# Later loads of s and b, first parts and splits of down 1 inside block 5, and a second product's weights in three steps, in an attention kernel with two FFNs

## The chip, the cores and the metric

The kernel runs on one core of a Trainium2 chip (trn2). The metric is device time in microseconds, the median of three runs. The profile and all rows below are of one further execution, taken by the hardware profiler.

## The reference

Chunked attention (4 batches, 8 heads, 768 tokens, chunks of 32 with 16 tokens to the left, 8 to the right and 8 memory tokens) gives a 3072 x 512 array. Two FFNs follow, the second one without a part in this change:

```python
h = x @ w_in                     # 3072x512 @ 512x2048
g = s * relu(h)**2 + b           # s and b are single numbers
x = g @ w_out                    # 3072x2048 @ 2048x512
h = x @ w2_in
x = (h - tanh(h)) @ w2_out
```

## The kernel before

**Stages.** Attention is done in 24 units of 128 tokens, and "up 1" (`x @ w_in`, relu, square, times `s`) in six blocks of 512 tokens with 16 tiles `t` each. The first two blocks and most of the attention stand in a hand-written order, the string `START`, whose tokens name a step and its index: `qk2` loads q and k of unit 2, `vv3` loads v of unit 3, `ra3` loads the raw weights 3 of `w_in` (64-bit numbers, which L131 to L145 turn into float32). The rest of up 1 is a loop over blocks `j` and tiles `t`. In both, each engine runs its instructions in the order in which the code issues them, and all DMAs go through one queue, SP's; a load on that queue also waits until the eighth load before it has landed.

**A tile of up 1** is 12 matmuls (`up1_products`), the relu on ScalarE (L398), and the square on VectorE (L408). After four tiles, `up1_combine` makes the sums that the next stage wants (four instructions of VectorE, L423) and `up1_store` writes all to DRAM.

**Down 1** (`g @ w_out`, the class `Down`) is a Strassen-like scheme of seven products P1, P6, P5, P7, P3, P2, P4. Each product has 12 entries, counted here from 0 at the first entry of P1, so that P6 begins with entry 12. An entry is 12 matmuls (`multiply`: two column groups, two row tiles, and three matmuls for each, since a float32 operand is held as a high and a low part: high times high, low weight times high, high times low). So an entry's third matmul is the first to need the low half of its data.

- A part is half of a product's data of a group of tokens, loaded from DRAM in two DMAs (L579); four buffers (`stream`). A part serves two entries.
- `split(i)` makes high and low of entry `i`: ScalarE adds `b` and writes the high half (L522), VectorE writes the low half (L523). Three buffers (`ring`), so `split(i + 2)`, which the code issues ahead of `multiply(i)`, can only start once entry `i - 1` is through. The ring lies where weights 4 and 5 of `w_in` and the high halves of block 5's input were; splits 0, 1 and 2 take these places in this order.
- `weights(p, half)` makes the weights of a product: up to two sums (L489, L504), the high half on ScalarE (L508), the low half (L509). For P6 all but the high half is done on VectorE, for the later products on GpSimd (POOL).
- `run` loads the first four parts, does splits 0 and 1, and then goes through the entries.

From entry 11 of P1 on, only TensorE's order is by hand; the other engines' order is set by a scheduler when the kernel is built.

Of the kernel before, what the change touches and what calls it, by code (L numbers as in the profile page):

```python
# [11 lines left out]
AF = mybir.ActivationFunctionType  # L12
# [5 lines left out]
P = 128  # L18
# [40 lines left out]
def tile_chunk_attention_two_ffn(  # L59
# [12 lines left out]
    nc = tc.nc  # L72
    NU = qk.shape[0]
    UB = NB // P
    NBLK = NT // NB
# [27 lines left out]
    def new(place, n, dt, name):  # L103
        assert n <= SIZE[place[0]], (place, n)
        if place[0] in "QSRY":
            assert place[0] in side["letters"], place
        pool = arena if place[0] in "EZ" else side["of"]
        return pool.tile([P, n], dt, tag=place, name=name)
# [12 lines left out]
    b_c = const.tile([P, 1], F32, name="b_c")  # L121
# [95 lines left out]
    def load_qk(u):  # L217
        qk_t[u] = new(A_QK0[u] if u < 5 else A_QK[(u + 1) % 3], 1280, F32, "qk")
        nc.sync.dma_start(out=qk_t[u], in_=qk[u])
# [45 lines left out]
    def divide(u):  # L265
        sm, sums = sm_t[u], sum_t.pop(u)
        rs = small.tile([P, 8, 1], F32, tag="rs", name="rs")
        nc.vector.tensor_scalar_add(sums, sums, 1e-9)
        nc.vector.reciprocal(out=rs.rearrange("p h o -> p (h o)"), in_=sums)
        nc.vector.tensor_tensor(out=sm, in0=sm, in1=rs.to_broadcast([P, 8, KE]), op=ALU.mult)  # L270
# [51 lines left out]
    def att_step(i):  # L322

        if i - 1 < NU:
            transposes(i - 1)
            copies(i - 1)
        if i - 2 < NU:
            values(i - 2)
            x_high(i - 2)
            if i + 1 < NU:  # L330
                load_v(i + 1)
        if i < NU:
            scores(i)
            if i + 3 < NU:
                load_qk(i + 3)
        if i - 2 < NU:
            x_low(i - 2)
        if i < NU:
            mask(i)
            maximum(i)  # L340
            exponentials(i)
# [45 lines left out]
    def up1_products(j, t, lo=0, hi=NB):  # L387

        n, i = t // 2, t % 2
        xh, xl = (x[:, :, lo:hi] for x in x_t[j])  # L390
        wh, wl = wi[1, n]
        ps = up_ps[j, t] = bank(5 + (16 * j + t) % 3)
        for c in range(KD):
            three(ps[:, lo:hi], wh[:, i, c, :], wl[:, i, c, :], xh[:, c, :], xl[:, c, :], c == 0, c == KD - 1)

    def up1_relu(j, t):
        r = up_r[j, t] = new(A_R[(16 * j + t) % 3], NB, F32, "r")
        nc.scalar.activation(out=r, in_=up_ps[j, t], func=AF.Relu)  # L398
# [14 lines left out]
    def up1_combine(j, q, half):  # L413
        combine(*(t.rearrange("p s k t -> p s (k t)") for t in oab[j, q]), nc.vector, half)

    def up1_store(j, q):
        oa, ob = oab.pop((j, q))
        nc.sync.dma_start(out=o1[j][:, q, 0:3], in_=oa[:, 1:4].rearrange("p s k t -> p s (k t)"))
        nc.sync.dma_start(out=o1[j][:, q, 3:7], in_=ob.rearrange("p s k t -> p s (k t)"))

    def combine(oa, ob, eng, half=None):

        sub = lambda o, x, y: eng.tensor_tensor(out=o, in0=x, in1=y, op=ALU.subtract)  # L423
        if half in (None, 0):
            sub(ob[:, 0], oa[:, 0], oa[:, 1])
            sub(ob[:, 1], oa[:, 2], ob[:, 0])
        if half in (None, 1):
            sub(ob[:, 2], oa[:, 2], oa[:, 0])
            sub(ob[:, 3], ob[:, 1], oa[:, 3])

    class Down:
# [48 lines left out]
                self.loaded += 1  # L480

        def weights(self, p, half, eng=nc.gpsimd):

            z = lambda k: self.z[k, half]
            name = ORDER[p]

            def combo(i, x, y, op):
                t = new(self.smap[i][half], 1024, F32, f"s{i}")
                eng.tensor_tensor(out=t, in0=x, in1=y, op=op)  # L489
                self.st[i, half] = t  # L490
                return t

            if name == "P1":
                src = z("A11")
            elif name == "P6":
                s1 = combo(0, z("A21"), z("A22"), ALU.add)
                src = combo(1, s1, z("A11"), ALU.subtract)
            elif name == "P5":
                src = self.st[0, half]
            elif name == "P7":  # L500
                src = combo(0, z("A11"), z("A21"), ALU.subtract)
            elif name == "P3":
                src = self.st[1, half]
                eng.tensor_tensor(out=src, in0=z("A12"), in1=src, op=ALU.subtract)  # L504
            else:
                src = z("A12" if name == "P2" else "A22")
            w = new(self.whl[p % 2][half], 2048, F32R, "whl")
            nc.scalar.activation(out=w[:, 0:1024], in_=src, func=AF.Copy)  # L508
            eng.tensor_tensor(out=w[:, 1024:2048], in0=src, in1=w[:, 0:1024].bitcast(F32), op=ALU.subtract)  # L509
            self.w[p, half] = tuple(  # L510
                w[:, 1024 * q:1024 * (q + 1)].rearrange("p (k m) -> p k m", k=4) for q in range(2)
            )
# [32 lines left out]
        def run(self, between):  # L545
            deep = len(self.stream)
            self.load_to(deep - 1)
            n = len(self.entries)
            for i in range(2):
                self.split(i)  # L550
            for i in range(n):
                if i + 2 < n:
                    self.split(i + 2)
                    if i % 2:
                        self.load_to(i // 2 + 1 + deep)
                self.multiply(i)
                p, k = divmod(i, 4 * NG)
                if p + 1 < 7 and k in (5, 9):
                    self.weights(p + 1, (k - 5) // 4, nc.vector if p == 0 and self.turn == 0 else nc.gpsimd)
                between(p, k)  # L560

    class Sums:
# [24 lines left out]
    def final1(name, g, ps):  # L587
# [29 lines left out]
        else:  # L617
# [3 lines left out]
    down1 = Down(  # L621
        wo1, Z1, B_S, B_WHL, B_STREAM, B_RING, load1,
        lambda part, e: part.rearrange("p (b k t) -> p b k t", b=2, k=4)[:, :, 2 * e:2 * e + 2].rearrange(
            "p b k t -> p b (k t)"
        ),
        lambda t: lambda k: t[:, :, HB * k:HB * (k + 1)],
        b_c[:, 0:1], final1, 0,
    )
# [14 lines left out]
    for token in START.split():  # L643
        name = token.rstrip("0123456789")
        steps[name](int(token[len(name):]))
        if token == "qk2":
            nc.sync.dma_start(out=s_c, in_=s.partition_broadcast(P))
            nc.sync.dma_start(out=b_c, in_=b.partition_broadcast(P))

    load_v(13)  # L650
    load_qk(15)
    load_v(14)
    load_qk(16)

    quads = []
    for j in range(2, NBLK):
        last = j == NBLK - 1
        for t in range(16):
            q, i4 = t // 4, t % 4
            step = i4 == 2 and not last  # L660
            if step:
                att_step(4 * j + 6 + q)
            if t in ((0, 5) if last else (0, 8)):
                quads.append(down1.load_quadrant(A_RAW[1 if last else q // 2]))
            up1_products(j, t)
            if t in ((4, 9) if last else (6, 14)):
                quads.pop().end()
            if step and 4 * j + 6 + q < NU:
                divide(4 * j + 6 + q)
            up1_relu(j, t)  # L670
            up1_square(j, t)
            if t in ((3, 8) if last else (4, 12)):
                quads[-1].begin()
            if last and t in (4, 10):
                down1.weights(0, t // 8, nc.vector)
                down1.load_to(t // 8)
            if i4 == 3:
                up1_combine(j, q, None)
                up1_store(j, q)

# [3 lines left out]
    def w2_load(n):  # L684
        w2[n] = load_raw(wi2, n, C_RAW[0])

    def w2_make(n):
        make_pair(w2.pop(n), C_Z, C_W[n % 2], 2, n)

    def between1(p, k):  # L690
        if p == 0 and k == 4 * NG - 1:
            region.close()
            region.enter_context(tc.manual_schedule(engines={nc.tensor.engine}))
        if p == 6 and k == 0:
            w2_load(0)
        if p == 6 and k == 6:
            w2_make(0)

    down1.run(between1)
    thunks = []  # L700

# [153 lines left out]
```

## Time and profile before

| | |
|---|---|
| median of 3 runs | 1096.37 us (1095.09 to 1096.51) |
| the profiled execution | 1096.79 us, of which the span of instructions is 1095.0 us |
| PE (TensorE) busy | 1064.3 us, 97% of the span, 6072 matmuls |
| DVE (VectorE) busy | 711.0 us, 65% |
| ACT (ScalarE) busy | 487.2 us, 44% |
| POOL (GpSimd) busy | 264.7 us, 24% |
| mean granted clock of TensorE | 0.995 |

The span is from the first instruction to the last. Shares are averages over stages that differ: what an engine limits has to be read from the stage.

### The profile page before, as it was taken

Reading aid. Unit: us, or ns where it says so; the run is one execution under the profiler, and the core shown is the slowest. Engines: PE = TensorE matmul, PEld = TensorE weight load, DVE = VectorE, ACT = ScalarE, POOL = GpSimd, SP = SyncE. Lnnn points to the kernel's source line nnn. Section 1 sums busy time; section 2 is a strip of 40 time slices with the busy share of each in tenths; the row PEclk is TensorE's granted clock in tenths of the full one; section 3 lists DMA queues with packets and bytes.
Section 4 is the critical chain, followed back from the end, with each engine's and each line's share of the span. In section 5 each row is a group of like instructions: output and inputs, shape, how many; then the busy total and the mean of one; then the engine's idle time right before and its main releaser. Section 6 shows DMA issues by size and latency. Waiting matters only on the chain.

```text
span 1095.0 us, 15206 instructions
## 1 busy us (share of the span) xinstructions
PE 1064.3 (97%) x6072; PEld 877.8 (80%) x6072; DVE 711.0 (65%) x742; ACT 487.2 (44%) x863; POOL 264.7 (24%) x164
## 2 busy tenths in 40 slices
PE   5899999999999889999999999999999999999998
PEld 4778888888888668888888888888888888888886
DVE  6897777777758596578779885323322566576654
ACT  6665564555523454445555333222222454444432
POOL 1000000000000061011101378655657951111100
PEclk8999999999999999999999999999999999999999
DMA  8874858666448745655565765555535966566751
GB/s 271 263 252 188 274 195 318 251 243 223 181 192 315 263 152 192 194 193 192 195 225 183 267 252 220 224 200 211 226 153 208 334 227 214 195 223 238 241 202 58
DMA packets 71687, 242.16 MB, mean 221 GB/s; under 512 B 5312, under 2 KB 5312, under 8 KB 61376
## 3 DMA queue, kind: packets, MB, share of 16 engines
q1 hardware_dynamic: 71616, 241.19, 61.7%
q8 instruction: 47, 0.77, 0.3%
q14 instruction: 24, 0.20, 0.1%
HBM read 146.80 MB, written 94.37 MB: 220 GB/s over the span
## 4 chain that ended last, share of the span: by engine, by line
PE 90%; DVE 4%; DMA 4%; issue 1%; ACT 0%; SPq 0%; DVEq 0%; ACTq 0%
PE pb L124 28%; PE pb L126 28%; PE pb L125 28%; DMA raw<-in_wi_dram 2%; DMA qk<-in_qk_dram 2%; PE pb L298 2%; PE pb L276 2%; PE pb L236 1%; DVE ringhringl L523 1%; DVE ob L423 1%; DVE oa L408 0%; DVE z L145 0%; DVE z L139 0%; DVE sm L270 0%; ACT z L131 0%
## 5 line engine op out<-in xcount | busy, mean ns | idle before, releaser
L126 PE MATMUL pb<-ringhringl,whl 128*128 128x512 f32 x560 | 219.7, 392 | 7.0 <-DVE ringhringl L523 7.0
L124 PE MATMUL pb<-ringhringl,whl 128*128 128x512 f32 x560 | 218.7, 391 | 1.7 <-ACT ringhringl L522 1.7
L125 PE MATMUL pb<-ringhringl,whl 128*128 128x512 f32 x560 | 218.6, 390 | 0.0
L528 DVE TENSOR_TENSOR ringhringl<-part,ringhringl 128x1024 fp32r<-128x1024 f32 x92 | 128.5, 1397 | 84.7 <-ACT ringhringl L527 84.7
L527 ACT ACTIVATE ringhringl<-part 128x1024 fp32r<-128x1024 f32 x92 | 97.7, 1062 | 135.6 <-PE pb L126 121.5
L124 PE MATMUL pb<-xh,w 128*128 128x512 f32 (+1 forms) x392 | 153.9, 393 | 2.3 <-DVE oa L408 2.2
L125 PE MATMUL pb<-xh,w 128*128 128x512 f32 (+1 forms) x392 | 151.3, 386 | 0.3 <-DVE w L378 0.3
L126 PE MATMUL pb<-xl,w 128*128 128x512 f32 (+1 forms) x392 | 151.3, 386 | 0.0
L126 PEld LDWEIGHTS pb<-ringhringl,whl 128*128 128x128 f32 x560 | 105.5, 188 | 32.1 <-DVE ringhringl L523 10.2
L768 DVE TENSOR_TENSOR oa<-pb,r 128x1024 f32<-128x1024 f32 x48 | 58.5, 1221 | 107.8 <-ACT r L767 103.6
L124 PEld LDWEIGHTS pb<-ringhringl,whl 128*128 128x128 f32 x560 | 105.5, 188 | 23.6 <-ACT ringhringl L522 2.1
L125 PEld LDWEIGHTS pb<-ringhringl,whl 128*128 128x128 f32 x560 | 105.4, 188 | 22.1
L504 POOL TENSOR_TENSOR s<-zq,s 128x1024 f32<-128x1024 f32 x4 | 12.5, 3114 | 383.1 <-DVE whl L509 383.0
L767 ACT ACTIVATE r<-pb 128x1024 f32<-128x1024 f32 x48 | 49.1, 1025 | 122.9 <-PE pb L126 122.4
L398 ACT ACTIVATE r<-pb 128x512 f32<-128x512 f32 x96 | 55.7, 592 | 100.1 <-PE pb L126 85.7
L523 DVE SCALAR_TENSOR_TENSOR ringhringl<-part,b_c,ringhringl 128x1024 fp32r<-128x1024 f32 x48 | 74.4, 1569 | 27.6 <-ACT ringhringl L522 27.6
L408 DVE SCALAR_TENSOR_TENSOR oa<-pb,s_c,r 128x512 f32<-128x512 f32 x96 | 70.1, 746 | 32.1 <-ACT r L398 32.1
L124 PEld LDWEIGHTS pb<-xh,w 128*128 128x128 f32 x392 | 73.6, 188 | 19.8 <-DVE oa L408 4.1
L125 PE MATMUL pb<-x2hx2l,w 128*128 128x512 f32 x224 | 87.2, 389 | 0.0
L126 PE MATMUL pb<-x2hx2l,w 128*128 128x512 f32 x224 | 87.2, 389 | 0.0
L124 PE MATMUL pb<-x2hx2l,w 128*128 128x512 f32 x224 | 87.2, 389 | 0.0
L260 ACT ACTIVATE sm<-sm,nmx 128x96 f32<-128x96 f32 x192 | 69.2, 365 | 37.7 <-DVE nmx L254 37.7
(108 smaller groups left out, 1818.0 us busy)
## 6 DMA issues: line engine op xcount, KB each, us to landing
o<-ob SPq DMA_DIRECT2D x48, 1024.0 KB, 4.7
part<-o SPq DMA_DIRECT2D x84, 512.0 KB, 4.6
part<-o SPq DMA_DIRECT2D x42, 1024.0 KB, 4.9
o<-oa SPq DMA_DIRECT2D x48, 768.0 KB, 3.4
raw<-in_wi_dram SPq DMA_DIRECT2D x16, 1024.0 KB, 6.6
raw<-in_wo_dram SPq DMA_DIRECT2D x16, 1024.0 KB, 7.2
qk<-in_qk_dram SPq DMA_DIRECT2D x24, 640.0 KB, 8.1
v<-in_vw_dram SPq DMA_DIRECT2D x24, 384.0 KB, 8.4
```

The lines of the kernel that those rows point to most:

```text
L124: nc.tensor.matmul(acc, lhsT=whi, rhs=xhi, start=first, stop=False)
L125: nc.tensor.matmul(acc, lhsT=wlo, rhs=xhi, start=False, stop=False)
L126: nc.tensor.matmul(acc, lhsT=whi, rhs=xlo, start=False, stop=last)
L260: nc.scalar.activation(out=sm[:, h, :], in_=sm[:, h, :], func=AF.Exp, bias=nmx[:, h:h + 1], scale=1.0, accum_out=sums[:, h:h + 1],)
L276: nc.tensor.transpose(out=bank(2 + g)[0:KE, P * r:P * (r + 1)], in_=sm[:, 4 * g + r, :], identity=ident)
L398: nc.scalar.activation(out=r, in_=up_ps[j, t], func=AF.Relu)
L408: nc.vector.scalar_tensor_tensor(out=oab[j, q][0][:, 2 * i:2 * i + 2, k, :], in0=ps2, scalar=s_c[:, 0:1], in1=r2, op0=ALU.mult, op1=ALU.mult,)
L523: nc.vector.scalar_tensor_tensor(out=xl, in0=src, scalar=self.bias, in1=xh.bitcast(F32), op0=ALU.add, op1=ALU.subtract)
L527: nc.scalar.activation(out=xh, in_=src, func=AF.Copy)
L528: nc.vector.tensor_tensor(out=xl, in0=src, in1=xh.bitcast(F32), op=ALU.subtract)
L767: nc.scalar.activation(out=r, in_=ps[:, :, 0:NB], func=AF.Tanh)
L768: nc.vector.tensor_tensor(out=oa[:, 2 * i:2 * i + 2], in0=ps[:, :, 0:NB], in1=r, op=ALU.subtract)
```

## The change

`s` is loaded behind v of unit 3 (so in front of v of unit 2), and `b` after the hand-written order. In the last block (block 5), parts 1 and 2 are loaded at tile 10 and part 3 at tile 11, and splits 0 and 1 are done at tiles 13 and 14. The block's last combine and store come after entry 0 of down 1, which is after split 2. P6's weights are made in three steps per half (`sums`, `high`, `low`), one entry apart, from entry 2 and from entry 6 on; before, all of a half came at entry 5 and at entry 9.

```diff
         def weights(self, p, half, eng=nc.gpsimd):
+            self.sums(p, half, eng)
+            self.high(p, half)
+            self.low(p, half, eng)
...
             self.load_to(deep - 1)
             n = len(self.entries)
             for i in range(2):
-                self.split(i)
+                if i not in self.xs:
+                    self.split(i)
...
                 p, k = divmod(i, 4 * NG)
-                if p + 1 < 7 and k in (5, 9):
-                    self.weights(p + 1, (k - 5) // 4, nc.vector if p == 0 and self.turn == 0 else nc.gpsimd)
+                if p == 0 and self.turn == 0:
+                    half = k // 6
+                    if k in (2, 6):
+                        self.sums(1, half, nc.vector)
+                    if k in (3, 7):
+                        self.high(1, half)
+                    if k in (4, 8):
+                        self.low(1, half, nc.vector)
+                elif p + 1 < 7 and k in (5, 9):
+                    self.weights(p + 1, (k - 5) // 4)
...
-        if token == "qk2":
+        if token == "vv3":
             nc.sync.dma_start(out=s_c, in_=s.partition_broadcast(P))
-            nc.sync.dma_start(out=b_c, in_=b.partition_broadcast(P))
...
     load_qk(16)
 
+    nc.sync.dma_start(out=b_c, in_=b.partition_broadcast(P))
...
                 down1.weights(0, t // 8, nc.vector)
-                down1.load_to(t // 8)
-            if i4 == 3:
+            if last and t in (4, 10, 11):
+                down1.load_to({4: 0, 10: 2, 11: 3}[t])
+            if last and t in (13, 14):
+                down1.split(t - 13)
+            if i4 == 3 and not (last and q == 3):
                 up1_combine(j, q, None)
                 up1_store(j, q)
...
     def between1(p, k):
+        if p == 0 and k == 0:
+            up1_combine(NBLK - 1, 3, None)
+            up1_store(NBLK - 1, 3)
```

How the engines' orders change, row by row. In these rows a line number is that of the file the rows are of: L523 (low half of a split) is L535 in the changed file, L489 (a sum) is L494, L504 (P3's sum) is L509, L509 (low half of weights) is L521. `x4` says that four such instructions follow one another.

VectorE from tile 12 of block 5 to entry 5 of down 1, before:

```order
L408 SCALAR_TENSOR_TENSOR oa<-pb,s_c,r 128x2x256 x4
L423 TENSOR_TENSOR ob<-oa 128x512
L423 TENSOR_TENSOR ob<-oa,ob 128x512
L423 TENSOR_TENSOR ob<-oa 128x512
L423 TENSOR_TENSOR ob<-ob,oa 128x512
L523 SCALAR_TENSOR_TENSOR ringhringl<-part,b_c,ringhringl 128x1024 x8
```

And now, from tile 12 to split 4:

```order
L408 SCALAR_TENSOR_TENSOR oa<-pb,s_c,r 128x2x256 x2
L535 SCALAR_TENSOR_TENSOR ringhringl<-part,b_c,ringhringl 128x1024
L408 SCALAR_TENSOR_TENSOR oa<-pb,s_c,r 128x2x256
L535 SCALAR_TENSOR_TENSOR ringhringl<-part,b_c,ringhringl 128x1024
L408 SCALAR_TENSOR_TENSOR oa<-pb,s_c,r 128x2x256
L535 SCALAR_TENSOR_TENSOR ringhringl<-part,b_c,ringhringl 128x1024
L423 TENSOR_TENSOR ob<-oa 128x512
L423 TENSOR_TENSOR ob<-oa,ob 128x512
L423 TENSOR_TENSOR ob<-oa 128x512
L423 TENSOR_TENSOR ob<-ob,oa 128x512
L535 SCALAR_TENSOR_TENSOR ringhringl<-part,b_c,ringhringl 128x1024 x2
```

Splits 0 and 1 now stand between the last squares, split 2 behind the last square, and the last combine between splits 2 and 3; before, all four instructions of the combine stood ahead of split 0.

VectorE over the entries of P1, before, from split 0 on:

```order
L523 SCALAR_TENSOR_TENSOR ringhringl<-part,b_c,ringhringl 128x1024 x8
L489 TENSOR_TENSOR s_3658<-zq 128x1024
L489 TENSOR_TENSOR s_3660<-s_3658,zq 128x1024
L509 TENSOR_TENSOR whl<-s_3660,whl 128x1024
L523 SCALAR_TENSOR_TENSOR ringhringl<-part,b_c,ringhringl 128x1024 x4
L489 TENSOR_TENSOR s_3733<-zq 128x1024
L489 TENSOR_TENSOR s_3735<-s_3733,zq 128x1024
L509 TENSOR_TENSOR whl<-s_3735,whl 128x1024
L523 SCALAR_TENSOR_TENSOR ringhringl<-part,b_c,ringhringl 128x1024 x6
```

And now, from split 3 on:

```order
L535 SCALAR_TENSOR_TENSOR ringhringl<-part,b_c,ringhringl 128x1024 x2
L494 TENSOR_TENSOR s_3605<-zq 128x1024
L494 TENSOR_TENSOR s_3607<-s_3605,zq 128x1024
L535 SCALAR_TENSOR_TENSOR ringhringl<-part,b_c,ringhringl 128x1024 x2
L521 TENSOR_TENSOR whl<-s_3607,whl 128x1024
L535 SCALAR_TENSOR_TENSOR ringhringl<-part,b_c,ringhringl 128x1024 x2
L494 TENSOR_TENSOR s_3680<-zq 128x1024
L494 TENSOR_TENSOR s_3682<-s_3680,zq 128x1024
L535 SCALAR_TENSOR_TENSOR ringhringl<-part,b_c,ringhringl 128x1024 x2
L521 TENSOR_TENSOR whl<-s_3682,whl 128x1024
L535 SCALAR_TENSOR_TENSOR ringhringl<-part,b_c,ringhringl 128x1024 x7
```

The second half's weights were done behind split 11 and are now done between splits 8 and 11, with splits 9 and 10 among their steps.

GpSimd's first instructions after its masks, of the second product (P6) and later, before and now, as one piece of the difference:

```order
-L504 TENSOR_TENSOR s_3660<-zq,s_3660 128x1024
-L509 TENSOR_TENSOR whl<-s_3658,whl 128x1024
-L489 TENSOR_TENSOR s_4089<-zq 128x1024
-L504 TENSOR_TENSOR s_3735<-zq,s_3735 128x1024
-L509 TENSOR_TENSOR whl<-s_3733,whl 128x1024
-L489 TENSOR_TENSOR s_4161<-zq 128x1024
+L509 TENSOR_TENSOR s_3607<-zq,s_3607 128x1024
+L509 TENSOR_TENSOR s_3682<-zq,s_3682 128x1024
+L521 TENSOR_TENSOR whl<-s_3605,whl 128x1024
+L494 TENSOR_TENSOR s_4089<-zq 128x1024
+L521 TENSOR_TENSOR whl<-s_3680,whl 128x1024
+L494 TENSOR_TENSOR s_4161<-zq 128x1024
```

These are P3's two sums (they work in place on P6's sums, so each must follow P6's low half), P5's low halves and P7's sums. Both of P3's sums now stand first.

## Rows read from the trace of the kernel before

**Rows 1.** Windows: core, stretch: us, busy us of each engine (instructions), clock, DMA share, GB/s.

```profile
150.00:300.00 150.00, 149.77 (x1278) 124.10 (x1277) 114.76 (x180) 78.34 (x257) 0.00 (x0) 1.00 0.68 247
365.00:367.70 2.70, 2.70 (x8) 2.08 (x8) 1.92 (x2) 0.00 (x0) 0.00 (x0) 0.55 0.98 250
```

**Rows 2.** What PE waited for, whole span: us in total, times, longest us.

```profile
PE pb L236 <- DMA qk<-in_qk_dram: 9.9, 6, 4.6
PE pb L126 <- DVE ringhringl L523: 7.0, 6, 3.0
```

**Rows 3.** Windows of the first 39 us, columns as in group 1.

```profile
7.00:10.00 3.00, 2.45 (x56) 1.93 (x48) 2.93 (x5) 1.66 (x9) 0.00 (x0) 1.00 0.26 87
12.40:22.60 10.20, 6.63 (x80) 5.30 (x80) 8.88 (x15) 8.45 (x32) 0.00 (x0) 0.84 1.03 306
22.60:38.70 16.10, 13.82 (x218) 12.50 (x219) 13.26 (x19) 10.49 (x28) 0.00 (x0) 0.89 1.02 281
```

**Rows 4.** Chain that ended last, 0 to 60 us: start us, us, what.

```profile
28.89 9.79 DMA raw<-in_wi_dram
```

**Rows 5.** Timeline of PE, block 5 to down 1: start us, us, instruction [idle before].

```profile
358.99 0.39 PE L126 MATMUL pb<-xl,w 128*128 128x512 f32 x1
361.10 0.50 PE L124 MATMUL pb<-ringhringl,whl 128*128 128x512 f32 x1 [1.73 <-ACT ringhringl L522]
...
364.58 0.80 PE L126 MATMUL pb<-ringhringl,whl 128*128 128x512 f32 x1 [2.74 <-DVE ringhringl L523]
...
367.61 0.39 PE L124 MATMUL pb<-ringhringl,whl 128*128 128x512 f32 x1
```

**Rows 6.** Timeline of PE, P1 to P6.

```profile
399.28 0.39 PE L125 MATMUL pb<-ringhringl,whl 128*128 128x512 f32 x1
402.66 0.50 PE L126 MATMUL pb<-ringhringl,whl 128*128 128x512 f32 x1 [2.99 <-DVE ringhringl L523]
...
405.29 0.39 PE L125 MATMUL pb<-ringhringl,whl 128*128 128x512 f32 x1
405.99 0.50 PE L126 MATMUL pb<-ringhringl,whl 128*128 128x512 f32 x1 [0.31 <-DVE ringhringl L523]
...
415.06 0.39 PE L124 MATMUL pb<-ringhringl,whl 128*128 128x512 f32 x1
```

**Rows 7.** Timeline of ACT, last tiles of block 5.

```profile
356.70 0.60 ACT L398 ACTIVATE r<-pb 128x512 f32<-128x512 f32 x1 [2.12 <-PE pb L126]
359.42 0.60 ACT L398 ACTIVATE r<-pb 128x512 f32<-128x512 f32 x1 [2.12 <-PE pb L126]
359.91 3.21 ACT L522 ACTIVATE ringhringl<-part,b_c 128x1024 fp32r<-128x1024 f32 x3
```

**Rows 8.** Timeline of DVE, end of block 5 into down 1.

```profile
357.33 0.75 DVE L408 SCALAR_TENSOR_TENSOR oa<-pb,s_c,r 128x512 f32<-128x512 f32 x1 [1.97 <-ACT r L398]
...
360.71 0.68 DVE L423 TENSOR_TENSOR ob<-oa 128x512 f32<-128x512 f32 x1
...
363.24 3.67 DVE L523 SCALAR_TENSOR_TENSOR ringhringl<-part,b_c,ringhringl 128x1024 fp32r<-128x1024 f32 x3
...
381.78 1.22 DVE L489 TENSOR_TENSOR s<-zq 128x1024 f32<-128x1024 f32 x1
```

**Rows 9.** DVE line L523: duration ns min/median/max, first and last start us.

```profile
L523 DVE SCALAR_TENSOR_TENSOR ringhringl<-part,b_c,ringhringl x48: 1271/1284/3442, 363.2 to 560.8; 128x1024 fp32r<-128x1024 f32 x48
```

**Rows 10.** Timeline of POOL, P1 to P6.

```profile
394.96 3.26 POOL L509 TENSOR_TENSOR whl<-s,whl 128x1024 fp32r<-128x1024 f32 x1 [4.87 <-ACT whl L508]
...
401.48 3.38 POOL L504 TENSOR_TENSOR s<-zq,s 128x1024 f32<-128x1024 f32 x1
```

**Rows 11.** POOL on tile zq, columns as in group 9.

```profile
L509 POOL TENSOR_TENSOR whl<-zq,whl x10: 2402/2511/3417, 499.1 to 1026.9; 128x1024 fp32r<-128x1024 f32 x10
```

**Rows 12.** Timeline of SP, the loads of down 1's parts.

```profile
346.18 0.88 SPq L579 DMA_DIRECT2D part<-o  x2
...
363.78 2.52 SPq L579 DMA_DIRECT2D part<-o  x3
```

More of the change, by code (lines that the diff above doesn't have):

```diff
@@ L482, in weights, with sums @@
         def weights(self, p, half, eng=nc.gpsimd):
+            self.sums(p, half, eng)
+            self.high(p, half)
+            self.low(p, half, eng)
+        def sums(self, p, half, eng):
             z = lambda k: self.z[k, half]
@@ L506, in weights, with high, low @@
                 src = z("A12" if name == "P2" else "A22")
+            self.w[p, half] = src
+        def high(self, p, half):
             w = new(self.whl[p % 2][half], 2048, F32R, "whl")
-            nc.scalar.activation(out=w[:, 0:1024], in_=src, func=AF.Copy)
+            nc.scalar.activation(out=w[:, 0:1024], in_=self.w[p, half], func=AF.Copy)
+            self.w[p, half] = (self.w[p, half], w)
+        def low(self, p, half, eng):
+            src, w = self.w[p, half]
             eng.tensor_tensor(out=w[:, 1024:2048], in0=src, in1=w[:, 0:1024].bitcast(F32), op=ALU.subtract)
```

## The prediction

> **What bounds the kernel now.** Read first the busy shares by stage. Between 150 and 300 us TensorE is busy 149.77 of 150 us [rows 1]: there the kernel is bound by matmuls, no edit touches that stage, and a shift of all that goes before it passes straight to the end. So the change can only work where TensorE waits. The list of its waits names two such places [rows 2]: 9.9 us for q and k at the start, and 7.0 us for the low halves of splits (`ringhringl`, L523) where down 1 begins. Then take each place from the timelines.
>
> Start. The queue of loads is what runs there: from 12.4 to 38.7 us the DMA engines are full (share 1.03 and 1.02). But from 7 to 10 us the share is 0.26 at 87 GB/s [rows 3], although the first three loads of q and k are all but through and large loads stand behind them; what lies between in the queue are `s` and `b`, a single number each, spread to 128 partitions. Against the 1.02 of the full stretch that hole is 3.0 x (1 - 0.26/1.02) = 2.2 us. The chain that ended last runs over the fourth load of raw weights, issued at 28.89 and 9.79 us under way [rows 4], so a full queue delays it, and behind it stand the conversions of weights that TensorE's first tiles need.
>
> Beginning of down 1. The last matmul of block 5 starts at 358.99; the next ten steps should take 10 x 0.227 = 2.27 us (a tile of 12 matmuls takes 2.72 us, by the relus of two tiles at 356.70 and 359.42 [rows 7]), but the tenth matmul from there starts at 367.61 [rows 5]. So 8.62 - 2.27 = **6.35 us** are lost. Why: ScalarE starts split 0 at 359.91, behind the last relu [rows 7]; VectorE first does the last square and the four instructions of the combine (from 360.71) and starts the low halves at 363.24 [rows 8]. The two idle gaps are 1.73 and 2.74 us [rows 5]; the rest is the clock, which fell behind these gaps: 0.55 granted between 365.0 and 367.7 [rows 1], about the lower of its two levels, 1.2 of 2.4 GHz.
>
> P1 to P6. From 367.61 (matmul 9 of down 1, counted from 0) to 415.06 (matmul 192, the first of entry 16) are 183 steps, 41.5 us at 0.2267, and 47.45 us pass [rows 5, 6]: **5.95 us** more are lost. The largest piece is entry 12: its second matmul starts at 399.28, the third, which needs the low half of its split, at 402.66 [rows 6]; on VectorE that split stands behind split 11 and the whole of P6's second half. Entries 13 to 15 lose about 0.6 us each in the same place (405.29 to 405.99, less a step and a little slow start [rows 6]), and entry 9 did once. Here VectorE and GpSimd hold each other up: a low half takes 1.28 us in the median but up to 3.44 [rows 9], and a tensor operation of GpSimd, 2.40 us at its shortest [rows 11], takes 3.26 to 3.38 [rows 10]. Five follow one another from 394.96, 3.34 us apart (one is that at 401.48); in each such period VectorE gets one operation, and TensorE wants a split every 2.72.
>
> **The change part by part, in the profiled execution's time (1096.79).**
>
> Start. The hole of `b` leaves the full stretch; its new place is near 160 us, where TensorE has loads in hand, so I cost it at nothing (if the cover were gone: 1.1 us). `s` stays in the full stretch, ahead of v of unit 2. Each had half of the hole, so q and k of unit 3 and the next loads come 2.2 us earlier, and what stands behind `s`, with the raw weights on the chain, 1.1 us. Bounds: 0 (something else made the hole, or it comes back whole) and 2.2 (in a queue with work on both sides a small load costs nothing). I take **1.1**, since the row shows the hole in just such a queue. On SP, v of unit 2 now waits also for the landing of the first raw weights; the queue is full long beyond that, so no cost.
>
> The Trainium skill speaks against this term: its page DMA: Bandwidth & Descriptors (Queues, rings and completion order) says that data descriptors of a ring are consumed in order and carry no barrier, so a load of 512 bytes should hardly hold what is behind it. By that the term would be 0 and the sum 1086.5; the row shows the engines idle, and I go by the row.
>
> Entry to down 1. In block 5 ScalarE idles 2.12 us per tile and VectorE 1.97 [rows 7, 8]; a split takes about 1.1 (a third of 3.21) on the one and 1.28 on the other, so splits 0 and 1 fit into tiles 13 and 14 at no cost. Count time T from the end of block 5's matmuls (359.2 before); entry i should start at 2.72 i, and its low half is due at 2.72 i + 0.45. Split 0 is then done at T = -2, split 1 at about 0.4 (due 3.2). Split 2 runs behind the last relu and square: high half to 1.7, low to 2.95, due 5.9. The combine (4 x 0.62 in a row) takes VectorE to 5.5, split 3 to 6.75, due 8.6. Parts 1 to 3 are issued from 346 on instead of 346.18 and 363.78 [rows 12], so none is late. No gap, so no fall of the clock either: **6.35** gained; at the least 4.47 (both gaps gone, the clock falls for another reason).
>
> P1 to P6. I carry the order on VectorE on, with 1.2 us per operation in a row (sums 1.22 [rows 8]); split i + 2 starts at 2.72 i at the earliest, and its high half takes 1.1 on ScalarE. Done / due: split 4 at 8.0 / 11.3; P6's first sums 10.4; split 5 at 11.7 / 14.0; split 6 at 15.4 / 16.8 (ScalarE has the high weights and P1's copy in between); low weights 16.6; split 7 at 17.8 / 19.5. Then GpSimd starts P3's first sum and holds split 8 to 21.1 / 22.2. Second sums 23.5, split 9 at 24.8 / 24.9, split 10 at 27.0 / 27.6, low weights 28.2, split 11 at 29.5 / 30.4. So entries 8 to 11 wait for nothing, two of them by a hair. At 28.3 GpSimd starts on five operations (P3's second sum, P5's two low halves and P7's two sums), and each split now comes 3.34 behind the last one: split 12 at 32.7 / 33.1, split 13 at 36.0 / 35.8, splits 14, 15 and 16 each 0.62 later than TensorE wants it. That is 0.2 + 3 x 0.6 = 2.0 us of waits where 5.95 were: **3.95** gained. Bounds: 5.95 (no waits left) and 2.5 (next paragraph's price of a period).
>
> With the shortest durations in the rows, one of each engine in turn, a period is 2.40 + 1.28 = 3.68 instead of 3.34 [rows 9, 11]; then the waits are about 3.5, the gain 2.5 and the sum 1086.9. The Trainium skill's page SBUF — State Buffer (SBUF: two separate sides) has a rule that leads there: whichever of the two engines starts first holds their shared port for its whole instruction. The measured periods are shorter, and I go by them.
>
> Sum: 1.1 + 6.35 + 3.95 = 11.4; 1096.79 - 11.4 = 1085.4. The median of the runs lies 0.42 below the profiled execution; I say **1085.2** for the median.
>
> **The rivals.**
>
> 1. Start gives nothing, or VectorE's tight entries 9 and 10 slip. For it: margins of 0.1 and 0.6 us; the rule on descriptors. Each collision with GpSimd costs 0.6 (as entry 9 before). One or both: 1086.5 to 1088.5.
> 2. The waits of P1 to P6 are as long as before, since GpSimd's five operations in a row are still there: 1096.8 - 7.45 = 1089.3. Against it: the largest one, 3.4 us of entry 12, came from VectorE's own order, which is changed.
> 3. `s` costs nothing in its new place and GpSimd's series begins late enough to leave a split in hand: up to 2.2 + 6.35 + 5.95, down to 1082.
> 4. The edits in block 5 don't do what they say: split 0 waits for its part or its place, and the gaps stay. Part 0 is loaded at tile 4 as before and its place was last read at tile 9; I see nothing that would hold it. With the gaps there, about 1091.7.
> 5. Slower: part 1 comes late. Split 2 stands on ScalarE and VectorE ahead of splits 3 and 4, the combine and P6's sums, so all would wait. It is issued near 346 and must land by T = 2.7 (361.9) to cost nothing; each microsecond behind that costs one. To end 2.2 us slower it would have to land 13.6 us later than that, near 375. Against it: it was issued at 346.18 before too, and was no bound.
>
> **How the numbers follow.** Forecast, 1083.5 to 1086.5: 0.62. Rival 1: 0.17 (1086.5 to 1088.5). Rival 2: 0.06. Rival 3 below 1083.5: 0.09. Rival 4: 0.04. Rival 5: 0.02. A range from 1082.5 to 1088.5 leaves out rivals 2, 4 and 5 and a part of 3, about 0.15. A difference of 0.2% (2.2 us) is about what a measurement here can tell from none. Faster by more: 0.95, the same 0.03, slower 0.02.
>
> **What would show it.** Start: no window near 7 to 10 us with a share below 0.5, but a smaller hole later, and TensorE's first tiles about 1 us earlier. Entry: no idle of TensorE between the last tile and entry 0, and a clock of 1.00 there. P1 to P6: no wait at entry 12 itself, and three or four of about 0.3 us idle (0.6 lost) at the third matmuls of entries 13 to 16. I am wrong if the list of waits still has one of 1 us or more at `ringhringl`, or if the first blocks don't move.

## The result and the profile after

The changed kernel takes **1081.15 us** in the median of four runs (1080.99 to 1081.83), the kernel before 1096.29 (1095.09 to 1096.51): a ratio of 0.9865, 95% interval 0.9848 to 0.9882. That is faster, and below the predicted range. The profiled execution took 1080.99 us (span 1079.2), so 15.8 us have gone where 11.4 were forecast.

**Waits.** TensorE's list over the whole span (what it waited for: us in total, times, longest), against [rows 2]:

```profile
PE pb L236 <- DMA qk<-in_qk_dram: 5.7, 2, 4.7
...
PE pb L126 <- DVE ringhringl L535: 0.9, 3, 0.3
```

The waits for q and k fall from 9.9 to 5.7 us, those for low halves from 7.0 to 0.9. Windows of the kernel after (columns as in [rows 1]):

```profile
7.00:10.00 3.00, 2.86 (x72) 2.33 (x68) 2.93 (x5) 1.56 (x9) 0.00 (x0) 1.00 1.03 431
20.00:30.00 10.00, 7.52 (x180) 6.47 (x180) 9.77 (x16) 9.66 (x29) 0.00 (x0) 1.00 0.89 249
27.00:28.00 1.00, 0.59 (x18) 0.47 (x18) 1.00 (x3) 1.00 (x3) 0.00 (x0) 1.00 0.10 41
36.00:37.00 1.00, 1.00 (x8) 0.87 (x7) 1.00 (x3) 0.59 (x1) 0.00 (x0) 1.00 0.14 54
150.00:300.00 150.00, 149.78 (x1279) 124.13 (x1278) 111.29 (x172) 75.57 (x241) 0.00 (x0) 1.00 0.68 245
360.00:375.00 15.00, 15.00 (x68) 12.43 (x67) 12.54 (x10) 7.86 (x8) 3.28 (x1) 1.00 0.97 336
375.00:390.00 15.00, 15.00 (x67) 12.11 (x66) 13.99 (x9) 10.54 (x11) 8.16 (x3) 1.00 0.46 155
390.00:400.00 10.00, 9.06 (x38) 6.49 (x37) 10.00 (x4) 4.39 (x4) 8.36 (x3) 1.00 0.58 192
```

The hole from 7 to 10 us (0.26 in [rows 3]) is a share of 1.03 now. And the queue is not full up to 38.7 us any more: at 27 to 28 and at 36 to 37 us it is nearly empty, because it waits for the next loads of raw weights to be issued (at 27.11 and at 36.45 us). From 150 to 300 us nothing is different, as it should be. Into down 1 TensorE is busy all the time at clock 1.00, where 0.55 stood in [rows 1]; only from 390 to 400 is a microsecond idle.

**Where the 15.8 us come from** is read off four marks: the last relu of block 5, the copy of the sum behind entry 3, the sum behind entry 19 (20 entries), and the end. Timelines of ScalarE and VectorE, of the kernel before and then of the kernel after:

```profile
376.67 1.03 ACT L605 ACTIVATE sumX<-pb 128x1024 f32<-128x1024 f32 x1 [1.57 <-PE pb L126]
426.14 1.22 DVE L603 TENSOR_TENSOR sumU<-sumX,pb 128x1024 f32<-128x1024 f32 x1 [0.25 <-PE pb L126]
```

```profile
33.87 0.59 ACT L398 ACTIVATE r<-pb 128x512 f32<-128x512 f32 x1
...
353.75 0.60 ACT L398 ACTIVATE r<-pb 128x512 f32<-128x512 f32 x1 [1.08 <-PE pb L126]
364.63 1.03 ACT L626 ACTIVATE sumX<-pb 128x1024 f32<-128x1024 f32 x1 [1.56 <-PE pb L126]
410.33 1.22 DVE L624 TENSOR_TENSOR sumU<-sumX,pb 128x1024 f32<-128x1024 f32 x1 [0.25 <-PE pb L126]
```

| stretch | before | after | gained | forecast |
|---|---|---|---|---|
| up to the last relu of block 5 | 359.42 [rows 7] | 353.75 | **5.67** | 1.1 |
| to the copy behind entry 3 | 17.25 | 10.88 | **6.37** | 6.35 |
| to the sum behind entry 19 | 49.47 | 45.70 | **3.77** | 3.95 |
| from there to the end of the span | 668.86 | 668.87 | 0 | 0 |

Four entries of 2.72 us are 10.88: the entry to down 1 loses nothing any more. Sixteen are 43.52, so 45.70 leaves 2.2 us lost, where 2.0 were forecast. The two terms of down 1 were right to 0.2 us. The start was not: 5.67 instead of 1.1, and 5.67 is more than the 2.2 that I had taken for its upper bound.

**The order in down 1**, timelines of TensorE, VectorE and GpSimd of the kernel after:

```profile
353.33 0.39 PE L126 MATMUL pb<-xl,w 128*128 128x512 f32 x1
353.55 0.39 PE L124 MATMUL pb<-ringhringl,whl 128*128 128x512 f32 x1
```

```profile
355.43 1.29 DVE L535 SCALAR_TENSOR_TENSOR ringhringl<-part,b_c,ringhringl 128x1024 fp32r<-128x1024 f32 x1 [0.29 <-ACT ringhringl L534]
...
359.16 2.50 DVE L535 SCALAR_TENSOR_TENSOR ringhringl<-part,b_c,ringhringl 128x1024 fp32r<-128x1024 f32 x2
361.58 1.22 DVE L494 TENSOR_TENSOR s<-zq 128x1024 f32<-128x1024 f32 x1
...
374.56 1.21 DVE L494 TENSOR_TENSOR s<-zq 128x1024 f32<-128x1024 f32 x1
```

```profile
381.76 3.31 POOL L509 TENSOR_TENSOR s<-zq,s 128x1024 f32<-128x1024 f32 x1 [8.21 <-DVE whl L521]
385.03 3.38 POOL L521 TENSOR_TENSOR whl<-s,whl 128x1024 fp32r<-128x1024 f32 x1
...
395.16 3.27 POOL L494 TENSOR_TENSOR s<-zq 128x1024 f32<-128x1024 f32 x1
```

Down 1's first matmul now starts one step behind block 5's last, and that is the forecast's T = 0. Split 2 ends at T = 3.2 (forecast 2.95), split 4 at 8.1 (8.0), P6's first sums begin at 8.0 (8.0) and the second ones at 21.0 (21.1), and GpSimd's five operations begin at 28.2 (28.3), 3.35 us apart. What they leave is three waits, in TensorE's timeline, 3.34 us apart where an entry takes 2.72; they are the third matmuls of entries 14 to 16:

```profile
392.89 0.50 PE L126 MATMUL pb<-ringhringl,whl 128*128 128x512 f32 x1 [0.31 <-DVE ringhringl L535]
396.22 0.50 PE L126 MATMUL pb<-ringhringl,whl 128*128 128x512 f32 x1 [0.32 <-DVE ringhringl L535]
399.57 0.50 PE L126 MATMUL pb<-ringhringl,whl 128*128 128x512 f32 x1 [0.32 <-DVE ringhringl L535]
```

### The profile page after: what moved, and what is told of

Same layout as the page of the kernel before. It is cut to its first block, busy times and chain, and to the rows that moved or that the text cites. A ratio compares the mean times of both kernels' runs of the same rounds, so it can differ in the third digit from the quotient of the medians.

```text
span 1079.2 us, 15211 instructions
## 1 busy us (share of the span) xinstructions
PE 1060.4 (98%) x6072; PEld 876.1 (81%) x6072; DVE 711.6 (66%) x742; ACT 486.6 (45%) x863; POOL 265.1 (25%) x164
## 4 chain that ended last, share of the span: by engine, by line
PE 91%; DVE 5%; ACT 2%; DMA 2%; issue 1%; DVEq 0%; ACTq 0%; SPq 0%
PE pb L124 29%; PE pb L126 29%; PE pb L125 29%; PE pb L298 2%; PE pb L276 2%; PE pb L236 1%; DMA raw<-in_wi_dram 1%; ACT sm L260 1%; DVE ringhringl L535 1%; DVE ob L423 1%; DVE oa L408 0%; DVE z L145 0%; DVE w L378 0%; DVE nmx L254 0%; DMA qk<-in_qk_dram 0%
## 5 line engine op out<-in xcount | busy, mean ns | idle before, releaser
L509 POOL TENSOR_TENSOR s<-zq,s 128x1024 f32<-128x1024 f32 x4 | 12.4, 3093 | 374.8 <-DVE whl L521 374.7
L535 DVE SCALAR_TENSOR_TENSOR ringhringl<-part,b_c,ringhringl 128x1024 fp32r<-128x1024 f32 x48 | 76.7, 1613 | 22.2 <-ACT ringhringl L534 21.9
L126 PEld LDWEIGHTS pb<-xl,w 128*128 128x128 f32 x392 | 73.6, 188 | 15.7 <-DVE xl L320 0.8
```

Source lines behind the costliest of these rows:

```text
L126: nc.tensor.matmul(acc, lhsT=whi, rhs=xlo, start=False, stop=last)
L535: nc.vector.scalar_tensor_tensor(out=xl, in0=src, scalar=self.bias, in1=xh.bitcast(F32), op0=ALU.add, op1=ALU.subtract)
```

## The experiments

Times are medians; each ratio is to runs of the kernel before on the same chip (its medians there 1095.2 to 1095.9), with a 95% interval. "Last relu" is that of block 5 in the profile.

### The three parts one by one

**Loads alone** (before, with only `s` and `b` moved as in the change) and **`b` alone** (`s` stays where it was):

```diff
-        if token == "qk2":
+        if token == "vv3":
             nc.sync.dma_start(out=s_c, in_=s.partition_broadcast(P))
-            nc.sync.dma_start(out=b_c, in_=b.partition_broadcast(P))
...
+    nc.sync.dma_start(out=b_c, in_=b.partition_broadcast(P))
```

> The kernel before with nothing changed but the places of the loads of s and b. If the third of the gain that I had sized wrongly is all from these two loads, it takes 5.6 us off (about 1090.7) and the raw weights 5 are issued near 41.4 us instead of 46.8. The rival, that block 5 or down 1 gave part of it, leaves about 1 us here (1095).

> The kernel before with b late and s still third in the queue. Theory A, each small load at the front of the queue stops it for about 1.1 us and the loss grows later: about half of the gain, 2.8 us off (1093.5), and a hole of half the size near 8 us. Theory B, s costs as much in its new place as in the old one, so that all of the gain is b's: 5.6 us off (1090.7).

Loads alone: 1092.63 us, 0.9971 (0.9960 to 0.9981), so 3.3 us less, last relu at 354.06. `b` alone: 1094.09, 0.9983 (0.9972 to 0.9994), 1.8 us less, last relu at 355.44. So each load taken from the front gives about half of the gain, and both together about 3.3, not 1.1 and not 5.7.

**Changed kernel with the loads where they were:**

> The changed kernel with s and b loaded third and fourth, as before. If the start is the part that my sum sized wrongly, this one gains what I gave the other two parts, 10.3 us, and no more (about 1085.5 to 1086); if the loads only alone, 3.3 us, and the changed kernel, 14.7, are to be believed, 11.4 (1084.5). The rival, that the start gives 5.6 us in all runs, leaves 9.5 (1086.5).

1084.04, 0.9898 (0.9878 to 0.9918): 2.9 us above the changed kernel, or 3.4 if each is set against the runs of before on its own chip. The loads' gain is about the same whether down 1 is changed or not. The hole is back (windows of this kernel):

```profile
7.00:10.00 3.00, 2.21 (x56) 1.75 (x48) 2.93 (x5) 1.66 (x9) 0.00 (x0) 1.00 0.17 53
```

**Entry alone** (parts, splits 0 and 1, and the last combine as in the change; loads and weights as before) and **weights alone** (only the three steps of P6's weights). Of the first, against the changed kernel:

```diff
-                if p == 0 and self.turn == 0:
...
-                elif p + 1 < 7 and k in (5, 9):
-                    self.weights(p + 1, (k - 5) // 4)
+                if p + 1 < 7 and k in (5, 9):
+                    self.weights(p + 1, (k - 5) // 4, nc.vector if p == 0 and self.turn == 0 else nc.gpsimd)
```

> The kernel before with the early loads of parts, splits 0 and 1 in block 5 and the late combine, but with P6's weights in one piece at entries 5 and 9 and the loads of s and b as before. By my sum 6.35 us off and the wait at entry 12 still there: about 1089.5, TensorE waits of 2.5 to 3.5 us at the low halves of splits. The rival: with entry 0 earlier, the waits of P1 to P6 grow by what the entry gave, since VectorE has the same work in less time; then 1093 or more.

> The kernel before with only P6's weights in three steps. By my sum 3.95 us off (1092), the 6.35 us behind block 5 still lost, and 0.9 more where the clock had fallen behind the wait at entry 12. The rival: with splits 0 to 2 late, VectorE has no room and the steps only move the wait: no change.

Entry alone: 1088.33, 0.9932 (0.9914 to 0.9950), 7.5 us less; the stretch to the copy behind entry 3 is 10.88, that to the sum behind entry 19 is 49.46, as before. Weights alone: 1091.75, 0.9961 (0.9945 to 0.9977), 4.1 us less; that stretch is 45.69, as in the changed kernel. TensorE's timeline of entry alone keeps the 3 us wait of entry 12 (402.66 in [rows 6]):

```profile
392.78 0.50 PE L126 MATMUL pb<-ringhringl,whl 128*128 128x512 f32 x1 [2.98 <-DVE ringhringl L535]
```

The timeline of weights alone keeps the two gaps at the entry (1.73 and 2.74 in [rows 5]) and has no other up to 400 us:

```profile
358.37 0.50 PE L124 MATMUL pb<-ringhringl,whl 128*128 128x512 f32 x1 [1.72 <-ACT ringhringl L534]
361.85 0.80 PE L126 MATMUL pb<-ringhringl,whl 128*128 128x512 f32 x1 [2.74 <-DVE ringhringl L535]
```

So each part does what was said of it, and they add up: 3.3 + 7.5 + 4.1 = 14.9 of the 15.1 between the medians.

What the old waits cost is not fixed, though. The two gaps at the entry are alike in all seven profiles that have them, but TensorE's granted clock behind them is not. From the last relu to the copy behind entry 3 the kernel before took 17.25 us and weights alone 18.36 (windows of the one, then of the other):

```profile
359.42:376.67 17.25, 12.82 (x49) 10.22 (x50) 10.69 (x11) 7.16 (x7) 0.00 (x0) 0.90 0.86 309
356.69:375.05 18.36, 13.94 (x49) 10.99 (x50) 12.34 (x13) 7.16 (x8) 0.00 (x0) 0.81 0.87 314
```

The other five lie at 17.29 to 17.52 (clock 0.90) and at 18.30 (0.81). In the stretch behind it, two of the seven profiles with the old weights lost 0.9 us more than the rest (50.4 instead of 49.5); in these two the clock fell furthest behind the wait of entry 12. So in some executions the old waits cost up to 1.1 us more at the entry, or 0.9 more at entry 12, than in the profile that the sum was made against.

### Why the start gave more than forecast

**Does `s` cost something in its new place?** The changed kernel with `s` loaded three times there:

```diff
             nc.sync.dma_start(out=s_c, in_=s.partition_broadcast(P))
+            nc.sync.dma_start(out=s_x, in_=s.partition_broadcast(P))
+            nc.sync.dma_start(out=s_y, in_=s.partition_broadcast(P))
```

> The changed kernel with s loaded three times, one behind the other, in the new place; the two further copies are read by nobody. Theory A, a small load in the middle of a full queue costs next to nothing: within 1 us of 1081.2. Theory B, each costs what it cost at the front: two further ones add about 5 us (1086). My prediction's price of 1.1 each: 1083.4.

1081.37, 0.9873 (0.9857 to 0.9889), last relu at 353.59: no cost. This is the step that failed. Its window from 20 to 26 us has a share of 0.87, where the changed kernel has 1.05:

```profile
20.00:26.00 6.00, 4.06 (x106) 3.44 (x106) 5.80 (x10) 6.00 (x24) 0.00 (x0) 0.98 0.87 237
```

So the loads still make holes there, but nobody waits for what is behind them. The queue is ahead of its users by then, as the empty stretch at 27 to 28 us of the changed kernel shows.

**Two more in front** (before, with two extra loads of `s` behind the first two):

```diff
             nc.sync.dma_start(out=b_c, in_=b.partition_broadcast(P))
+            nc.sync.dma_start(out=s_x, in_=s.partition_broadcast(P))
+            nc.sync.dma_start(out=s_y, in_=s.partition_broadcast(P))
```

> The kernel before with two further loads of s right behind the loads of s and b, read by nobody. If each small load at the front blocks the queue by itself, the hole from 7 to 10 us is twice as long and the time rises by about 5 us (1101.5). If the hole is a single delay that any number of small loads share, nothing changes (1096.3).

1097.15, 1.0015 (1.0004 to 1.0026): 1.25 us more in the median, between the two forecasts, last relu at 359.0. So more of these loads at the front cost more, but there is no fixed price for each: the first two cost 3.3. The hole does grow with them, to 2.7 + 1.5 = 4.2 us by the same sum as in the prediction, where two loads leave 2.2 to 2.5:

```profile
7.00:10.00 3.00, 2.25 (x56) 1.80 (x48) 2.93 (x5) 1.56 (x9) 0.00 (x0) 1.00 0.09 16
10.00:12.00 2.00, 0.00 (x0) 0.00 (x0) 1.74 (x6) 2.00 (x12) 0.00 (x0) 1.00 0.25 85
```

**The kernel before, once more:**

> The kernel before once more, for a second profile. If its start differs from one execution to the next, the last relu of block 5 is 1 to 3 us away from the 359.42 us of the first profile, and the rate in the full queue between 20 and 30 us is another; if the start is fixed, it is within 0.3 us.

1094.29 us, last relu at 356.68 where the first profile had 359.42. Windows of this second execution, and below them one of the first:

```profile
7.00:10.00 3.00, 2.42 (x56) 1.86 (x48) 2.93 (x5) 1.54 (x9) 0.00 (x0) 1.00 0.17 50
20.00:30.00 10.00, 9.35 (x132) 7.73 (x128) 9.20 (x16) 9.46 (x34) 0.00 (x0) 1.00 1.03 275
```

```profile
20.00:30.00 10.00, 7.46 (x117) 5.88 (x115) 9.20 (x15) 9.51 (x32) 0.00 (x0) 0.69 1.04 241
```

The hole is there in both, but from 20 to 30 us the full queue moved 275 GB/s in one and 241 in the other. Against this second execution the start gained 2.93 us, the entry 6.64 and P1 to P6 3.74. So 2.7 of the 5.67 us are the profiled execution's own late start. The three other profiles with `s` and `b` in front on this queue bear that out: their last relus are at 355.93 (entry alone), 356.69 (weights alone) and 356.75 (changed kernel with the loads where they were). Why the full queue was slower in it is open. TensorE's clock doesn't explain it: from 20 to 26 us it was 0.50 there and 1.00 in the second execution, but 0.50 in entry alone too, whose last relu is the earliest of these.

**`s` later still** (changed kernel, behind `vv5` instead of `vv3`):

> The changed kernel with s not loaded behind v of unit 3 but behind v of unit 5, still later. Theory A, the first 40 us are now set by the conversions on VectorE and the exponentials on ScalarE, and a small load behind the front costs nothing: 1080.7 to 1081.7, first relu of up 1 within 0.5 us of 33.87. Theory B, s still holds the queue where it is, as the prediction priced it: about 1.1 us less, 1080.0, with the first relu near 32.8.

1081.82 (1081.07 to 1084.51), 0.9869 (0.9853 to 0.9884), first relu of up 1 at 33.90 where it was 33.87. No gain, so `s` holds nobody at `vv3`. From 27 to 28 us the queue is as empty as in the changed kernel (share 0.11), and `s` is issued only at 27.93, so that stretch is not a hole made by `s`. The profiled execution, the longest of the four, lost its time later, at raw weights that came late (waited for until 58.38 us, in the changed kernel until 55.11).

**The small loads on another queue** (before, with both issued by ScalarE at the same place of the program):

```diff
-            nc.sync.dma_start(out=s_c, in_=s.partition_broadcast(P))
-            nc.sync.dma_start(out=b_c, in_=b.partition_broadcast(P))
+            nc.scalar.dma_start(out=s_c, in_=s.partition_broadcast(P))
+            nc.scalar.dma_start(out=b_c, in_=b.partition_broadcast(P))
```

> The kernel before with s and b loaded at the same place of the program, but issued by ScalarE into its own DMA queue. Nothing else is changed. Theory A, the small loads block only the queue that they stand in (what is behind them there waits for them): then the loads of q and k go on, no stretch near 7 to 10 us has a share below 0.8, the last relu of block 5 starts near 353.8 as with the new places, and the time is about 1092.6 as with the new places alone. Theory B, the small loads hold the DMA engines themselves, whatever the queue: a stretch with a share below 0.5 as before, last relu near 356.7 or later, 1095 to 1096.

1094.43, 0.9986 (0.9977 to 0.9995), last relu at 356.01: 1.3 us less, between the two. Its windows:

```profile
2.00:7.00 5.00, 0.69 (x17) 0.70 (x20) 0.00 (x0) 0.94 (x1) 1.38 (x12) 1.00 0.70 221
7.00:10.00 3.00, 2.21 (x56) 1.83 (x48) 1.97 (x3) 0.00 (x0) 0.00 (x0) 1.00 0.97 394
```

The hole from 7 to 10 us is gone, but now the stretch ahead of it, in which the first q and k are loaded, moves 221 GB/s where the changed kernel has 363, and TensorE starts at 6.30 instead of 4.70 us. ScalarE has nothing ahead of the two loads and issues them at 0.74 us, so they met the first loads. Theory A is right that the queue behind is free; it missed that the loads beside are slowed.

**One address or 128?** In the changed kernel two extra loads of one number per partition stand where `s` and `b` were, but each partition's number comes from a row of its own (`s` and `b` themselves are where the change puts them):

```diff
+        if token == "qk2":
+            nc.sync.dma_start(out=s_x, in_=qk[20][:, 0:1])
+            nc.sync.dma_start(out=s_y, in_=qk[21][:, 0:1])
```

> The changed kernel with two extra loads of one number to each of 128 partitions where s and b were before (behind the third load of q and k), but each partition's number comes from its own row of an input (5120 bytes apart) instead of the same number for all. The two tiles are read by nobody. Theory A, the hole is made by loads of 128 rows of 4 bytes as such: a share below 0.5 in 7 to 10 us and about 1084.0, as with s and b themselves at that place. Theory B, the hole is made by 128 reads of one and the same address: no share below 0.8 there, and 1081.0 to 1081.8 as the changed kernel.

1081.27, 0.9872 (0.9856 to 0.9889), last relu at 353.85: no cost, and no hole in its windows:

```profile
7.00:10.00 3.00, 2.21 (x74) 1.79 (x70) 2.93 (x5) 1.65 (x9) 0.00 (x0) 1.00 1.06 418
```

With `s` and `b` at this place the same window has a share of 0.17 and the time is 1084.04. Size, place, queue and number of the two loads are alike, and so is the number of packets (two extra loads of either kind add 288); what differs is where they read, one number for 128 partitions or 128 rows 5120 bytes apart. So it is not the smallness of a load that holds the queue, but the reading of one number by all partitions. No run separates the shared address itself from the place in memory of the two arrays `s` and `b`.

### What is left in P1 to P6

**P5's and P7's weights on VectorE** (changed kernel; GpSimd keeps P3's sums):

```diff
-                    self.weights(p + 1, (k - 5) // 4)
+                    self.weights(p + 1, (k - 5) // 4, nc.vector if self.turn == 0 and p in (1, 2) else nc.gpsimd)
```

> The changed kernel with the weights of P5 and P7 made on VectorE instead of GpSimd, so that GpSimd has no five operations in a row beside the splits. Theory A, the three waits of 0.3 us idle (0.6 lost) at entries 13 to 15 come from VectorE and GpSimd holding each other up: they go, and the time falls by 1.5 to 2.0, to 1079.2 to 1079.7, with the stretch between the first copy of sums and the second sum 1.5 to 2 us shorter than 45.70. Rival, VectorE is then too full (each period of 2.72 us holds a split of 1.28 and an operation of 1.22): other waits at the splits, 1081 or more.

(The waits stand at entries 14 to 16, as shown above, not at 13 to 15.)

**1079.48** (1078.90 to 1080.03), 0.9849 (0.9836 to 0.9863): the best of all, 1.7 us below the changed kernel. Its timelines:

```profile
365.76 1.03 ACT L626 ACTIVATE sumX<-pb 128x1024 f32<-128x1024 f32 x1 [1.56 <-PE pb L126]
409.32 1.22 DVE L624 TENSOR_TENSOR sumU<-sumX,pb 128x1024 f32<-128x1024 f32 x1 [0.25 <-PE pb L126]
```

Between the two marks 43.56 us pass, 16 entries to 0.04, and `ringhringl` is gone from the list of waits. TensorE from 390 to 400, where 9.06 stood:

```profile
390.00:400.00 10.00, 10.00 (x46) 8.29 (x45) 9.45 (x9) 5.54 (x6) 0.00 (x0) 1.00 0.69 219
```

VectorE is busy 9.45 of these 10 us, and that is enough: alone, a split and a sum take 1.28 + 1.22 = 2.50 us of an entry's 2.72. So the 2.2 us that were left came from the two engines holding each other up.

## Why the prediction was wrong, point by point

- **Entry to down 1: right.** 6.35 forecast, 6.37 measured, no gap and no fall of the clock. Entry alone keeps all other waits and gains this one. In the medians it gave 7.5; a likely reason is that the profile of the sum had the cheapest fall of the clock of all seven (17.25 us, up to 18.36 in others).
- **P1 to P6: right.** 3.95 forecast, 3.77 measured, and the waits left are those forecast, in size and place (entries 14 to 16), with GpSimd's five operations at their time. Taking these away gave 2.1 us in this stretch.
- **GpSimd beside VectorE.** The period came out at 3.35 us, as in [rows 10], not at the 3.68 that the shortest rows and the rule of the Trainium skill's SBUF — State Buffer (SBUF: two separate sides) lead to. The measurement decides: of the two shortest durations, 2.40 and 1.28 us, about 0.33 ran side by side, if these are what each takes alone.
- **Start: wrong, and it is this step that failed:** "`s` stays in the full stretch, ahead of v of unit 2. Each had half of the hole, so q and k of unit 3 and the next loads come 2.2 us earlier, and what stands behind `s`, with the raw weights on the chain, 1.1 us." The halves were right (`b` alone gave 1.8, both 3.3). But I charged `s` its half again in the new place, and three of them there cost nothing. I took the "full" share up to 38.7 us for a limit that would stay. It was the hole's own consequence: without it the loads of the first 27 us are through early, and the queue runs empty. The chain that ended last, 0 to 60 us (as in [rows 4]), shows what bounds the start instead. In the second execution of the kernel before, it consists of loads from 3.3 to 30.6 us:

```profile
3.31 8.90 DMA qk<-in_qk_dram
...
12.22 18.41 DMA v<-in_vw_dram
```

In the kernel after, it has no load between 4.7 and 41.4 us; ScalarE's exponentials and VectorE's work fill that time:

```profile
0.75 3.91 DMA qk<-in_qk_dram
...
8.44 5.84 ACT sm L260 x32
...
41.37 6.28 DMA raw<-in_wi_dram
```

So it is in five of the six profiles with both loads moved back on SP's queue (in the sixth, P5's and P7's weights on VectorE, loads of raw weights and v are on the chain), and in none of those with both in front on SP's queue. The 9.79 us of the raw weights in [rows 4] belong to the first execution. In the second they were issued at 29.46 and taken up 6.75 us later (6.6 to 7.0 in the other three with both loads in front), in the kernel after at 27.11 and 5.70 later. Timelines of SP and ScalarE, before and then after:

```profile
29.46 0.35 SPq L348 DMA_DIRECT2D raw<-in_wi_dram  x1
...
36.21 1.17 ACT L131 ACTIVATE z<-raw 128x1024 f32<-128x1024 f32 x1 [1.75 <-DMA raw<-in_wi_dram]
```

```profile
27.11 0.33 SPq L348 DMA_DIRECT2D raw<-in_wi_dram  x1
...
32.81 1.16 ACT L131 ACTIVATE z<-raw 128x1024 f32<-128x1024 f32 x1 [1.50 <-DMA raw<-in_wi_dram]
```

So 2.35 us come from the earlier issue, about the 2.2 of the hole, and 1.05 from a shorter load, whose queue is nearly empty when it starts (share 0.10 from 27 to 28 us). Of these 3.4 us at the first relu of up 1, 2.9 are left at the last relu of block 5.

- **The bound above was too low as well.** The hole in the profile I read was 2.2 us; in the second execution it is 3.0 x (1 - 0.17/1.02) = 2.5, and the start gains 2.9 against it, since the shorter load comes on top. The first execution had lost 2.7 us more, nearly all of it by the first relu of up 1 (39.83 against 37.29), in a queue that looked full. A sum made against one execution takes over such a loss: in all comparisons the runs of before spread over 1093.4 to 1099.2, while the four of the changed kernel lie between 1081.0 and 1081.8.
- **The rule on descriptors.** The Trainium skill's DMA: Bandwidth & Descriptors (Queues, rings and completion order), descriptors consumed in order without a barrier, would have made the term 0. For loads from 128 rows that is what was measured; for the two of this kernel it was about 3 us. I was right to go by the row; but what the prediction calls a small load holds the queue by what it reads, not by its size.
- **The rivals.** None of them came about as a whole. The third, at 9 in 100, named half of the cause (`s` costs nothing); its other half did not happen (2.2 us of waits are left), and its lower end, 1082, is still above the 1081.15 measured.

In numbers: the median came out 4.05 us below the forecast. 2.0 of it are the start (3.1, between the 2.9 and 3.3 of the experiments, instead of 1.1). Another 1.3 is what entry and weights alone gave in medians beyond their terms (7.5 + 4.1 against 6.35 + 3.95), though not in their stretches of the profiles. The clock behind the old waits, which cost up to 1.1 and 0.9 us more in other profiles than in the one of the sum, is the likely place; that it is the whole of it is not shown. The rest, 0.7, is in the medians of before (1096.29 where the sum had begun at 1096.6; by its own terms, 1085.4 less 0.42, the forecast would have been 1085.0 and not 1085.2) and in what the three parts together gave beyond their single gains.

## What to carry to other kernels

A full queue is a limit only as long as what fills it is late; ask what the queue would do once the hole ahead of it is gone, before charging a moved load its price again. Numbers that are spread from one address to all partitions belong behind what the first stage needs, or are read from rows of their own. Counting an engine's order, instruction by instruction with durations from the rows, against due times hit its waits to about 0.2 us here, but a term at the start should be taken from two executions, not one.

## What the runs showed of the hardware

- Two loads of one number to 128 partitions at the front of SP's queue idled the DMA engines for some 2.2 to 2.5 us (a share of 0.17 to 0.26 over 3 us) and cost 2.9 to 3.3 us of time; two loads of as many bytes and packets from 128 rows cost nothing (share 1.06). On a queue of their own they slowed the loads beside them (221 against 363 GB/s from 2 to 7 us).
- At a share of 1.03 to 1.04, from 20 to 30 us, the same queue moved 241 GB/s in one execution and 275 in another.
- Behind the same two gaps at the entry to down 1, TensorE's mean granted clock over the next 17 to 18 us was 0.90 in five executions and 0.81 in two, which took up to 1.1 us longer.
- TensorE's granted clock fell behind the 3 us wait of entry 12 in some executions and not in others. With the loads alone it was 0.55 from 396 to 402 us (about the lower level, 1.2 of 2.4 GHz), and the stretch to the sum behind entry 19 took 50.39 instead of 49.47:

```profile
396.00:402.00 6.00, 4.53 (x11) 3.61 (x12) 6.00 (x3) 1.08 (x2) 6.00 (x3) 0.55 0.04 6
```
